# Windowed attention before a mixture of experts: scores computed in quarters of the tensor array, and a step of the attention rearranged

## The chip, the cores and the metric

The kernel runs on one core of a Trainium2 chip. The metric is the device time of one execution in microseconds (us). The engines are named as the profile names them: PE is TensorE (PEld are its weight loads), DVE is VectorE, ACT is ScalarE, POOL is GpSimd, and SP issues most of the DMAs. Each engine works through its own queue in order; an instruction that has to wait holds up everything behind it on its engine. Matmul results go to PSUM, which has eight banks of 128 partitions x 512 float32.

## What is computed

An attention with a causal window of 64 positions (8 batches, 8 heads, 576 positions, 64 features a head) is followed by a mixture of eight experts, of which each token takes one:

```python
scores = scale * np.matmul(q, k.transpose(0, 1, 3, 2))
rel = pos[:, None] - pos[None, :]
mask = (rel >= 0) & (rel < window)
scores = np.where(mask, scores, -1000000000.0)
attn = np.exp(scores - np.max(scores, axis=-1, keepdims=True))
attn = attn / (np.sum(attn, axis=-1, keepdims=True) + 1e-09)
out = np.matmul(attn, v)                      # -> x: 4608 tokens x 512
...
logits = x @ w_gate + modality_bias[modality_id]
e_idx = np.argmax(logits, axis=1)             # one expert of 8 for a token
...
h = np.maximum(x[mask] @ w1[e], 0.0)          # 512 -> 1024
out[mask] = gate_w[mask, None] * (h @ w2[e])  # 1024 -> 512
```

## The kernel before, in words

**Tiling.** The 4608 tokens are 72 blocks of 64 tokens; three blocks are a group (24 groups). The main loop (L922) has one step g for each block, and a few more to drain what is under way; `j` is g modulo 3. In each step several blocks are at different stages: `scores` of block g, `probs_t` (transposed probabilities) of block g - 1, `values` (probabilities times v) of block g - 2, and `x_t` (the result's rows transposed, for the gate) of block g - 3. Once in a group come `logits` and `logits_sum` (j = 0) and the ranks of the tokens among their experts (`route2`, `route3`, j = 2), after which the rows go to a table in DRAM, sorted by expert.

**The order is written out by hand.** Every engine gets its instructions in the order in which the loop's functions issue them. Small VectorE instructions for tables and routing wait in lists and go out one at a time where the loop calls `tick`.

**Transposed heads.** For a group, `load_qk` fetches q and k in four parts (K0, K1, Q0, Q1: k or q, first or last four heads), with two neighbouring tokens of a head beside each other, which is a run of 512 bytes in DRAM. `heads_t` transposes a part with four products into a bank `tp`. `heads_out` copies it out in two instructions of 64 partitions x 384, one for even and one for odd tokens. Parts of the next group are done while the present one is computed; the tuple `PARTS` (L467) says in which step.

**Scores.** q goes to `qbd`, where two heads stand on the diagonal of a 128x128 matrix and the rest is zero (cleared once, L826). One product of full size with `kT` then gives the scores of two heads over the window's 128 keys (L545, four products a step; each is two instructions for float32). VectorE adds the mask, scales, and takes the row minima (L551, four times); ScalarE takes the exponentials with their sums (L563, four times, two of them early in the step and two at its end).

**Banks of PSUM.** `ps_t` has two banks (`tp`: transposed heads, logits, ranks), `ps_s`, `ps_p` and `ps_a` one each (`sp` scores, `pp` transposed probabilities, `ax` values in its first 256 columns and transposed rows in the last 256), and `ps_m` three (`em`, `y0`, `y1`), which belong to the experts. As long as no expert's work is under way, odd steps borrow `em` for the scores and `y1` in place of `ax` (`spare_bank`, L473).

**The experts' work.** A slot is 256 tokens of one expert; its work is cut into sixteen pieces of TensorE (`slot_pieces`): transposes of the rows (`x_part`), products with w1 (`first`) and with w2 (`second`). From step 23 on (FIRST) each step of the attention does two pieces (`gap`), so the rest of the attention and the first slots share TensorE; behind the attention the remaining slots run alone. What a piece leaves in PSUM is taken out by entries of the list `later`, which `run_later` issues; a relu on ScalarE (L285) and a subtraction on VectorE (L286) for a pair of `first`, a split into two parts (L190, L191) for `x_part`, a scaling by the gate (L307) for the last `second`. Inside the attention `bank` gives `em` to all but the second `x_part` of a slot, which takes a `tp` bank, or `em` too where `busy` is set (j = 0).

Of the kernel before, what the change touches and what calls it, by code (L numbers as in the profile page):

```python
# [26 lines left out]
def tile_window_attn_moe(  # L27
# [24 lines left out]
    TP = 2 * P          # tokens of a slot  # L52
# [21 lines left out]
    XBUF = 9  # L74
    LG = HP * GT // 2  # column of the logits in a bank behind transposed heads
# [13 lines left out]
    # source chunks of an expert's weights, each [128, WCH] in the layout of Whi/Wlo  # L89
# [6 lines left out]
    def load_piece(raw, ev, c):  # L96
        """Columns c of an expert's weights (ev: its index, a register value)."""
# [21 lines left out]
    routing = []        # goes first  # L119

    hold = []           # VectorE has something more urgent

    def tick(n=1, table=False):
        for _ in range(0 if hold and not table else n):
# [31 lines left out]
    def tiles_of(pool, nm, c, up, size):  # L156
        """floor(c / size), or with up ceil, of whole numbers."""
# [6 lines left out]
    # experts X and Y: one-hot, first block (less DUMMY), index  # L164
# [4 lines left out]
    def first_max(pool, nm, c, out=None):  # L169
        """One-hot of the first maximum of c [1, E], and E minus its index."""  # L170
# [10 lines left out]
    def per_expert(pool, nm, c, xs_=slice(0, 2)):  # L181
        """Numbers c [1, E] of X and Y."""
# [3 lines left out]
    # ---------------------------------------------------------------- expert slots  # L186
    chunk_cols = [a * HALF + u * P for a in range(2) for u in range(HP // 2)]
# [26 lines left out]
    busy = [False]      # banks of ps_t are wanted soon  # L214
# [707 lines left out]
    for g in range(NBLK + 6):  # L922
# [56 lines left out]
        if n_gap > 2:  # L979
            gap(it)  # L980
# [285 lines left out]
```

## Time and profile before

| | us |
|---|---|
| median of 3 runs | 694.17 (694.06 to 695.51) |
| span of the profiled execution, first to last instruction | 692.6 |
| TensorE busy in the span | 670.0 |
| VectorE busy | 418.2 |
| ScalarE busy | 324.9 |

The profile records one execution; its span begins with the first instruction and ends with the last, and the time of a run also holds what lies around it. Busy times are sums over all stages, and a matmul's recorded duration contains the latency of the array, so matmuls that follow each other closely overlap in the record. In a row of the timeline stand the start, the duration, the engine, the line, the operation with its output and inputs, the shapes, how many instructions were merged, and in brackets how long the engine sat idle before and who released it. In a row of a group stand, behind the shapes and the count, the busy time in us, the mean of one in ns, and the idle time before with its releasers. In the list of who waited for whom a row gives the total in us, the number of waits and the longest.

### The profile page before, as it was taken

The numbers are of one execution on the slowest core, as the hardware profiler recorded it, in microseconds if no ns is written. First come the engines' busy times: TensorE is split into PE (matmuls) and PEld (weight loads), VectorE is DVE, ScalarE is ACT, GpSimd is POOL, SyncE is SP. The second block draws the span as 40 slices with busy tenths as digits, with TensorE's granted clock in tenths as the row PEclk, the third lists the DMA queues.
The fourth block names the chain that finished last, engine by engine and source line by source line (L and its number), as shares of the span: only waits on it lengthen the run. The fifth ranks groups of instructions, "written<-read, shape, count | busy, mean of one in ns | idle before, by whom it ended". The sixth has DMA issues, their size and how long they took to land. (4 is left out here: it accounts for less than half of the span.)

```text
span 692.6 us, 16517 instructions
## 1 busy us (share of the span) xinstructions
PE 670.0 (97%) x5814; PEld 598.9 (86%) x5814; DVE 418.2 (60%) x1760; ACT 324.9 (47%) x1029; POOL 189.3 (27%) x355
## 2 busy tenths in 40 slices
PE   7989699999999999999999999999999999999996
PEld 5778579989899898899999889999999999899985
DVE  4899987788778676675665665222226222656621
ACT  5778776666665555555555511111115211555511
POOL 6125544454454332232221251100110011111101
PEclk9999989999999999999999999999999999999998
DMA  7777896665765544554443121820505050686400
GB/s 180 182 193 203 218 234 166 175 168 160 203 177 157 145 127 131 131 153 130 130 126 83 67 78 62 278 62 32 183 31 183 32 183 31 198 258 199 143 9 34
DMA packets 108184, 97.60 MB, mean 141 GB/s; under 512 B 44602, under 2 KB 81540, under 8 KB 107972
## 3 DMA queue, kind: packets, MB, share of 16 engines
q1 hardware_dynamic: 101668, 77.51, 41.0%
q0 software_dynamic: 6432, 19.03, 7.7%
q8 instruction: 46, 0.75, 0.5%
q14 instruction: 38, 0.31, 0.2%
HBM read 67.65 MB, written 24.08 MB: 132 GB/s over the span
## 5 line engine op out<-in xcount | busy, mean ns | idle before, releaser
L563 ACT ACTIVATE ss<-ss,mn 128x128 f32<-128x128 f32 x288 | 113.4, 398 | 17.3 <-DVE mn L551 16.1
L299 PE MATMUL y<-Whi,hh 128*128 128x512 f32 x288 | 119.3, 414 | 0.0
L299 PE MATMUL y<-Whi,hl 128*128 128x512 f32 x288 | 113.7, 395 | 0.0
L299 PE MATMUL y<-Wlo,hh 128*128 128x512 f32 x288 | 113.0, 392 | 0.0
L719 POOL DMA_INDIRECT xs_scratch<-xa,idx x72 | 70.9, 984 | 141.2 <-issue 83.6
L277 PE MATMUL em<-xh,Whi 128*128 128x256 f32 x392 | 101.7, 292 | 0.0
L310 POOL DMA_INDIRECT out_dram<-y,id x36 | 37.1, 1031 | 220.4 <-DVE y L307 171.4
L277 PE MATMUL em<-xh,Wlo 128*128 128x256 f32 x392 | 96.6, 279 | 0.0
L285 ACT ACTIVATE hh<-em 128x512 fp32r<-128x512 f32 x49 | 29.3, 598 | 128.8 <-PE em L277 128.8
L286 DVE SCALAR_TENSOR_TENSOR hl<-em,hh 128x512 fp32r<-128x512 f32 x49 | 33.9, 691 | 90.4 <-ACT hh L285 90.2
L277 PEld LDWEIGHTS em<-xh,Whi 128*128 128x128 f32 x392 | 73.7, 188 | 2.3
L577 ACT COPY pT<-pp 128x512 f32<-128x512 f32 x72 | 42.1, 584 | 70.0 <-PE pp L571 69.6
L277 PEld LDWEIGHTS em<-xh,Wlo 128*128 128x128 f32 x392 | 73.7, 188 | 0.9
L545 PE MATMUL sp<-kT,qbd 128*128 128x128 f32 x488 | 66.4, 279 | 3.7 <-DVE qbd L523 3.6
L299 PEld LDWEIGHTS y<-Whi,hl 128*128 128x128 f32 x288 | 54.0, 188 | 12.6
L545 PEld LDWEIGHTS sp<-kT,qbd 128*128 128x128 f32 x488 | 59.8, 193 | 5.6 <-DVE qbd L523 4.6
L277 PE MATMUL em<-xl,Whi 128*128 128x256 f32 x392 | 62.1, 280 | 0.0
L299 PEld LDWEIGHTS y<-Whi,hh 128*128 128x128 f32 x288 | 54.1, 188 | 8.1
L299 PEld LDWEIGHTS y<-Wlo,hh 128*128 128x128 f32 x288 | 54.2, 188 | 7.6
L551 DVE CUSTOM_DVE_ANT_0 ss<-sp,masks 128x128 f32<-128x128 f32 x244 | 57.8, 279 | 4.8 <-PE sp L545 3.9
L111 POOL TENSOR_TENSOR Wlo<-raw,Whi 128x512 fp32r<-128x512 f32 x32 | 41.2, 1289 | 70.2 <-ACT Whi L110 69.9
L529 DVE COPY kT<-tp 64x384 f32<-64x384 f32 x94 | 52.1, 555 | 6.9 <-PE tp L511 4.3
(265 smaller groups left out, 1341.1 us busy)
## 6 DMA issues: line engine op xcount, KB each, us to landing
xt<-xs_scratch SPq DMA_DIRECT2D x18, 520.0 KB, 4.2
qk<-in_k_dram SPq DMA_DIRECT2D x48, 192.0 KB, 3.2
qk<-in_q_dram SPq DMA_DIRECT2D x48, 192.0 KB, 3.0
ve<-vo SPq DMA_DIRECT2D x71, 128.0 KB, 3.6
vo<-in_v_dram SPq DMA_DIRECT2D x32, 256.0 KB, 3.8
raw<-in_moe_w_dram SPq DMA_DIRECT2D x32, 256.0 KB, 2.9
vo<-in_moe_w_dram SPq DMA_DIRECT2D x24, 256.0 KB, 3.5
xs_scratch<-xs_scratch SPq DMA_DIRECT2D x8, 520.0 KB, 6.6
```

The source lines that it names most:

```text
L111: lo_engine.tensor_tensor(out=Wlo[:, buf, cols], in0=raw, in1=Whi[:, buf, cols].bitcast(F32), op=ALU.subtract)
L277: nc.tensor.matmul(out=hb[:, i * TP:(i + 1) * TP], lhsT=w[:, buf, c0:c0 + P], rhs=x[:, c * TP:(c + 1) * TP], start=(n == 0), stop=(n == le ...
L285: nc.scalar.activation(out=hh, in_=hb, func=AF.Relu),
L286: nc.vector.scalar_tensor_tensor(out=hl, in0=hb, scalar=0.0, in1=hh.bitcast(F32), op0=ALU.max, op1=ALU.subtract)))
L299: nc.tensor.matmul(out=sl["y", t], lhsT=h[:, i * TP + t * P:i * TP + (t + 1) * P], rhs=w[:, buf, c0:c0 + DM], start=(k == 0 and n == 0), s ...
L310: ins = nc.gpsimd.indirect_dma_start(out=out, out_offset=bass.IndirectOffsetOnAxis(ap=sl["id"][:, t:t + 1], axis=0), in_=y, in_offset=None ...
L529: (nc.scalar.copy if ((nm, a), t) in SCALAR or a and G == 0 else nc.vector.tensor_copy)(out=dst, in_=sv.rearrange("d (h i) -> d h i", h=HP))
L545: nc.tensor.matmul(out=sp[:, hp * P:(hp + 1) * P], lhsT=qbd[:, 1 + j if G % 2 else 2 - j, hp, :], rhs=win[:, hp], start=True, stop=True)
L551: nc.vector.tensor_tensor_reduce(out=ss[:, hp, :], in0=sp[:, hp * P:(hp + 1) * P], in1=mask, scale=-1.0 / 8.0, scalar=3.0e38, op0=ALU.add, ...
L563: nc.scalar.activation(out=ss[:, hp, :], in_=ss[:, hp, :], func=AF.Exp, bias=mn[:, hp:hp + 1], scale=-1.0, accum_out=sm[:, hp:hp + 1])
L577: nc.scalar.copy(out=pT, in_=pp)
L719: ins = nc.gpsimd.indirect_dma_start(out=xs_half, out_offset=bass.IndirectOffsetOnAxis(ap=idx[:, j:j + 1], axis=0), in_=xg[j], in_offset=None)
```

## The change

- **Scores.** `qbd` and its clearing go; q is kept in `qT` as k is in `kT`. `scores` issues eight products of 64 partitions by 64 columns, each in a quarter of the array: the partition half `a` of the operands (four of the eight heads stand in each) chooses the rows and one of two banks, `c` the columns. The product of a head takes half the partitions of the output, so the scores of two heads again fill 128 partitions. `ps_s` has two banks for it; in odd steps before the slots it borrows `y0` and `y1`.
- **Transposed heads.** `load_qk` fetches all heads of q or of k for a group into one tile, by four DMAs with runs of 256 bytes, one for each token parity and each half of the heads. `heads_t` transposes pairs of heads (one of each half), and `heads_out` copies a part out in one instruction of 128 partitions x 384 in place of two of 64.
- **Banks.** `ps_t` has one bank in place of two. Before the slots `tp_bank` takes turns between it and `em`. `ax` always has the bank of `ps_a`. The second `x_part` of a slot takes `em` as the first does.
- **Order of a step.** A step now begins with logits (j = 2), `values` and `values_out` of block g - 2, then the ranks (j = 1), `scores`, `probs_t`, all four exponentials, the first piece, the transposed heads, `x_t` and `x_t_out` of the same block g - 2, the second piece, and the second part of transposed heads. The loop is one step shorter. The device that held small VectorE instructions back (`hold`) goes, and `tick` is called with other counts.
- **Buffers.** Eight buffers `xa` in place of nine, three tiles of q and k in place of four of half the size, two in place of three of some small tables. The order of the features in the result's rows changes with the order of the heads (`chunk_cols`, `logits`).

```diff
-    ps_t = actx.enter_context(tc.tile_pool(name="ps_t", bufs=2, space=PSUM))
+    ps_t = actx.enter_context(tc.tile_pool(name="ps_t", bufs=1, space=PSUM))
...
-    qbd = att.tile([P, GB + 1, HP, P], F32, name="qbd")
+    qT = att.tile([P, HP, 6, W64], F32, name="qT")
...
-    SCALAR = ((Q0, 0), (Q0, 1))
-    LOADS = (0, 1, 1, 2)
-    HOLDJ = (2,)
-
-    def spare_bank(g):
-        """The slots' banks serve every other block as long as there is no slot."""
-        return g % 2 and g < FIRST - 1
+    SCALAR = (Q1,)
+    LOADS = (0, 1)
+
+    def early(g):
+
+        return g < FIRST - 1
+
+    n_tp = [0]
+
+    def tp_bank(g):
+        n_tp[0] += early(g)
+        if n_tp[0] % 2 and early(g):
+            return ps_m.tile([P, 512], F32, name="em")
+        return ps_t.tile([P, 512], F32, name="tp")
...
+        t = work.tile([GT // 2, HP, 2, 2, D], F32, name="qk", bufs=3)
+        src = (q_v if nm == "q" else k_v)[b, n]
+        for i in range(2):
+            for a in range(2):
+                nc.sync.dma_start(out=t[:, :, i, a, :], in_=src[:, a * HP:(a + 1) * HP, i])
...
+        src = qk[G, nm]
+        for h in range(2):
+            for t in range(2):
+                n = 2 * h + t
+                turn(tp[:, n * 96:(n + 1) * 96], src[:, 2 * i + h, t].rearrange("p a d -> p (a d)"))
...
+        dst = (qT if nm == "q" else kT)[:, 2 * i:2 * i + 2, pos0:pos0 + GB, :]
+        (nc.scalar.copy if (nm, i) in SCALAR or G == 0 and nm == "q" else nc.vector.tensor_copy)(
+            out=dst.rearrange("p h j (i t) -> p h t (j i)", t=2),
+            in_=tp[:, 0:4 * 96].rearrange("p (h t i) -> p h t i", h=2, t=2))
+        tick()
...
-        for hp in range(HP):
-            nc.tensor.matmul(
-                out=sp[:, hp * P:(hp + 1) * P], lhsT=qbd[:, 1 + j if G % 2 else 2 - j, hp, :], rhs=win[:, hp],
-                start=True, stop=True)
+        for s in range(2):
+            for a, c in ((0, 0), (1, 1), (0, 1), (1, 0)):
+                rows = slice(a * W64, (a + 1) * W64)
+                hp = 2 * c + s
+                nc.tensor.matmul(
+                    out=sp[a][c * W64:(c + 1) * W64, s * P:(s + 1) * P], lhsT=qT[rows, hp, p0, :],
+                    rhs=kT[rows, hp, p0 - 1:p0 + 1, :] if p0 else kT[rows, hp, 5::-5, :],
+                    start=True, stop=True)
```

The step's order after the change:

```diff
+        G2 = (g - 5) // GB if j == 2 else -1
+        R = (g - 7) // GB if j == 1 else -1
+        if G2 >= 0:
+            lt = tp_bank(g)
+            logits(G2, lt)
+        ax = ps_a.tile([P, 512], F32, name="ax")
+        if 2 <= g < NBLK + 2:
+            new_x(g - 2)
+            values(g - 2, ax)
+            values_out(g - 2)
+        if G2 >= 0:
+            logits_sum(G2, lt)
+            route1(G2)
...
+            tp = tp_bank(g)
+            rk = route2(R, tp)
...
+        if g < NBLK:
+            scores(g)
...
+        if 1 <= g <= NBLK:
+            probs_t(g - 1)
+            probs_out(g - 1)
+        if g < NBLK:
+            exps(g, range(HP))
+        if n_gap > 0:
+            gap(it, True)
+        part, part2 = PARTS[j]
+            heads_out(heads_t(G + 1, *part, tp_bank(g)), G + 1, *part)
...
+        if 2 <= g < NBLK + 2:
+            x_t(g - 2, ax)
+            x_t_out(g - 2, ax)
         if n_gap > 1:
             gap(it)
+        tick(2)
         if more and part2:
+            heads_out(heads_t(G + 1, *part2, tp_bank(g)), G + 1, *part2)
```

More of the change, by code (lines that the diff above doesn't have):

```diff
@@ L119, in tile_window_attn_moe @@
     routing = []
-    hold = []
     def tick(n=1, table=False):
-        for _ in range(0 if hold and not table else n):
+        for _ in range(n):
             if routing and not table:
@@ L247, in x_part @@
                     return
-            tp = ps_t.tile([P, 512], F32, name="tp") if i and not busy[0] else bank(2)
+            tp = bank(2)
             cs_ = range(2 * i, 2 * i + 2) if nb == 2 else range(NC1)
@@ L544, in scores @@
-        for hp in range(HP):
-            nc.tensor.matmul(
-                out=sp[:, hp * P:(hp + 1) * P], lhsT=qbd[:, 1 + j if G % 2 else 2 - j, hp, :], rhs=win[:, hp],
-                start=True, stop=True)
+        if g % 2 and early(g):
+            sp = [ps_m.tile([P, DM], F32, name=f"y{a}") for a in range(2)]
+        else:
+            sp = [ps_s.tile([P, 512], F32, name=f"sp{a}") for a in range(2)]
+        for s in range(2):
[6 more added lines that the diff above has]
+                    start=True, stop=True)
@@ L840, in tile_window_attn_moe @@
     nc.gpsimd.memset(masks[:, 1, 0, :], NEG)
+    nc.gpsimd.tensor_copy(out=ident_r, in_=ident)
     nc.gpsimd.memset(first_oh, 0.0)
@@ L927, in tile_window_attn_moe @@
         more = G + 1 < NG and g < NBLK
-        if j in HOLDJ:
-            hold.append(True)
-        if g < NBLK:
-            scores(g)
-            exps(g, (0, 1))
-        busy[0] = j == 0 and g < NBLK + 6
-        if n_gap > 0:
-            gap(it, True)
-        busy[0] = False
-        part, part2 = PARTS[j]
-        tp = heads_t(G + 1, *part) if more and part else ps_t.tile([P, 512], F32, name="tp")
-        G2 = (g - 6) // GB if j == 0 else -1
+        G2 = (g - 5) // GB if j == 2 else -1
+        R = (g - 7) // GB if j == 1 else -1
         if G2 >= 0:
-            lt = ps_t.tile([P, 512], F32, name="tp")
+            lt = tp_bank(g)
             logits(G2, lt)
-        R = (g - 8) // GB if j == 2 else -1
+        ax = ps_a.tile([P, 512], F32, name="ax")
[6 more added lines that the diff above has]
+            route1(G2)
         cnt = None
         if R >= 0:
+            tp = tp_bank(g)
             rk = route2(R, tp)
@@ L948, in tile_window_attn_moe @@
                 cnt = counts(R, tp)
+        if g < NBLK:
+            scores(g)
+        if R >= 0:
+            if cnt is not None:
+                cnt = counts_out(tab if R in (0, NG - 1) else pl, cnt)
+            route3(R, rk)
+        if 1 <= g <= NBLK:
[6 more added lines that the diff above has]
+        part, part2 = PARTS[j]
         if more and part:
[L950 to L953 removed]
+            heads_out(heads_t(G + 1, *part, tp_bank(g)), G + 1, *part)
         if 1 <= g <= NBLK:
@@ L956, in tile_window_attn_moe @@
             tick()
[L957 to L960 removed]
+        run_later()
+        tick(2)
         if 1 <= g <= NBLK:
             sums_inverse(g - 1)
[L963 to L966 removed]
         if 2 <= g < NBLK + 2:
[L968 to L973 removed]
+            x_t(g - 2, ax)
+            x_t_out(g - 2, ax)
         if n_gap > 1:
             gap(it)
[L976 to L994 removed]
+        tick(2)
+        if more and part2:
+            heads_out(heads_t(G + 1, *part2, tp_bank(g)), G + 1, *part2)
         for raw, n, c in raws:
@@ L1001, in tile_window_attn_moe @@
             raws.append((load_piece(raw, evs[n], c), n, c))
-        tick()
+        tick(4)
         if g == 1:
             select_bias()
-            nc.gpsimd.tensor_copy(out=ident_r, in_=ident)
         if g == 2:
```

149 lines of the change are left out of this document (46 added, 103 removed).

## The prediction

> **What bounds the kernel now.** The share of busy time comes first, then the windows by stage, because a step of the attention means one thing before the experts' pieces begin and another beside them.
>
> ```profile
> PE 670.0 (97%) x5814; PEld 598.9 (86%) x5814; DVE 418.2 (60%) x1760; ACT 324.9 (47%) x1029; POOL 189.3 (27%) x355
> ...
> 70.00:90.00 20.00, 15.05 (x171) 12.72 (x170) 18.10 (x104) 14.27 (x53) 10.09 (x13) 0.87 0.89 219
> ...
> 230.00:260.00 30.00, 30.00 (x310) 27.32 (x309) 21.98 (x99) 16.81 (x59) 10.90 (x20) 1.00 0.41 121
> ```
>
> TensorE is busy 97% of the span. The windows' columns are PE, PEld, DVE, ACT, POOL, clock, DMA share, GB/s. In the first 96 us (steps 0 to 22, no pieces; stage B below) VectorE holds 18.1 of 20 us and TensorE waits; from step 23 (stage C) TensorE never stops. Behind the attention (stage D) it does the pieces alone. The timeline of TensorE then gives the steps; a step starts with its scores (L545).
>
> ```profile
> 14.70 1.10 PE L545 MATMUL sp<-kT,qbd 128*128 128x128 f32 x8
> ...
> 73.19 1.16 PE L545 MATMUL sp<-kT,qbd 128*128 128x128 f32 x8 [1.16 <-DVE qbd L523]
> ...
> 74.61 0.53 PE L633 MATMUL tp<-xaT,wg 128*32 128x192 f32 x8
> 75.07 0.69 PE L600 MATMUL ax<-ve,pT 128*64 128x64 f32 x16
> 75.69 0.66 PE L571 MATMUL pp<-ident,ss 128*128 128x128 f32 x4
> ...
> 76.49 0.52 PE L644 MATMUL tp<-sel,part 128*64 128x8 f32 x6
> 76.94 1.16 PE L545 MATMUL em<-kT,qbd 128*128 128x128 f32 x8
> ...
> 95.74 1.08 PE L545 MATMUL sp<-kT,qbd 128*128 128x128 f32 x8
> ```
>
> Steps 2 to 22 take 95.74 - 14.70 = 81.0 us, 3.86 each. Where TensorE stands still there, the last thing it waits for is VectorE's copy of q into `qbd` (1.16 us at 73.19). In stage C a step is full:
>
> ```profile
> 253.22 1.06 PE L545 MATMUL sp<-kT,qbd 128*128 128x128 f32 x8
> 254.03 0.36 PE L277 MATMUL em<-xh,Whi 128*128 128x256 f32 x1
> ...
> 255.53 0.49 PE L511 MATMUL tp<-ident,qk 96*128 96x96 f32 x4
> 255.95 0.69 PE L600 MATMUL ax<-vo,pT 128*64 128x64 f32 x16
> ...
> 258.09 0.60 PE L571 MATMUL pp<-ident,ss 128*128 128x128 f32 x4
> 258.53 0.38 PE L617 MATMUL ax<-ident,xa 128*128 128x128 f32 x2
> 258.75 0.49 PE L511 MATMUL tp<-ident,qk 96*128 96x96 f32 x4
> 259.08 1.08 PE L545 MATMUL sp<-kT,qbd 128*128 128x128 f32 x8
> ```
>
> From start to start: scores 0.81, a piece 1.50, heads 0.42 or 0.33, probabilities 0.44, transposed rows 0.22; stage C has 49 steps (23 to 71).
>
> **The change, part by part.** *Scores.* Eight instructions of 128x128 weights (0.81 / 8 = 0.10 us each) become sixteen of 64x64 weights that stream as many columns. One after another they take 16 x 0.10 = 1.62 us; four at a time 0.41. No row has quarters; the nearest is the values' product, sixteen instructions with 64-column weights in two halves of the columns: 75.07 to 75.69, 0.62 us. I take 0.60 and keep 0.41 and 1.62 for the range. Stage C would win 0.21 x 49 = 10.3 us.
>
> The Trainium skill, TensorEngine Tiling (Array Packing), section Theoretical Speedup, allows a factor of two for each dimension of at most 64, which would be the 0.41 and a total 13 us below mine. Its section Key Properties says that a change of tiling mode drains TensorE, which speaks the other way. No run here shows either.
>
> *Copies of q and k.* Eight copies of 64x384 a group become four of 128x384: VectorE loses three of six at 0.56 us, ScalarE one of two at 0.51 (rows below). In stage B that takes about 0.56 us a step off VectorE, the present bound. What is late next is the order of the step.
>
> *The loop through ScalarE in stage B.* Now odd steps put `ax` into another bank (`spare_bank`) and the copy `xaT` stands before half of the exponentials. After the change there is one bank `ax`, its step begins with `values` into it and ends with `x_t_out` reading it, and ScalarE comes to `x_t_out` only behind `probs_out` and all four exponentials. `probs_out` waits for `probs_t`, which TensorE issues behind `values` and `scores`. So `values` of the next step waits for this step's `xaT`: a loop of one step. That waits go by bank and not by columns shows in who waited for whom:
>
> ```profile
> DVE xa L608 <- ACT xaT L624: 36.0, 31, 2.5
> ...
> DVE qbd L523 <- PE tp L690: 9.1, 9, 1.0
> ```
>
> L608 and L624 both only read `ax`, in different columns, and still one waits for the other; L690 writes columns of `tp` that L523 doesn't read. The durations:
>
> ```profile
> 41.12 0.66 PE L571 MATMUL pp<-ident,ss 128*128 128x128 f32 x4
> ...
> 41.81 0.59 ACT L577 COPY pT<-pp 128x512 f32<-128x512 f32 x1 [0.52 <-PE pp L571]
> ...
> 46.90 0.39 ACT L563 ACTIVATE ss<-ss,mn 128x128 f32<-128x128 f32 x1
> ...
> 47.29 0.39 ACT L563 ACTIVATE ss<-ss,mn 128x128 f32<-128x128 f32 x1
> ```
> ```profile
> L529 DVE COPY kT<-tp 64x384 f32<-64x384 f32 x94 | 52.1, 555 | 6.9 <-PE tp L511 4.3
> L624 ACT COPY xaT<-ax 128x256 f32<-128x256 f32 x62 | 23.6, 380 | 2.3 <-PE ax L617 2.3
> L523 ACT COPY qbd<-tp 64x384 f32<-64x384 f32 x46 | 23.3, 506 | 0.3
> ```
>
> An exponential follows the one before by 0.39, and a handover costs about 0.03 (41.12 + 0.66 to 41.81). Loop: values 0.62 + scores 0.60 + probabilities to their end 0.66 + `pT` 0.59 + four exponentials 1.56 and the last sum's read 0.10 (estimate) + `xaT` 0.38 + four handovers 0.12 = 4.63 us. The step j = 1 adds the rank's products, about 0.2 (82.36 to 82.55 below); j = 2 adds logits 0.46, their sum 0.45, and Q1's copy on ScalarE, 0.51, in front of `xaT`. A group is 3 x 4.63 + 0.2 + 1.42 = 15.5 us; the first has no logits yet, 14.4. Six of the one and one of the other: 107.4 us against 81.0, **26 us more**. VectorE (about 9 us a group: 18.1/20 of 11.6 less 1.7) and TensorE lie inside it.
>
> *Banks in stage C.* There the loop is shorter than TensorE's own work (3 x 4.63 against 5.2 and more a step) and costs nothing. But `ps_t` has one bank, and two places need it back at once. First, Q0's transposes end step j = 1 and the next step opens with `logits` into the same bank, which waits for VectorE's copy of Q0. The rows that it stands behind:
>
> ```profile
> L285 ACT ACTIVATE hh<-em 128x512 fp32r<-128x512 f32 x49 | 29.3, 598 | 128.8 <-PE em L277 128.8
> L286 DVE SCALAR_TENSOR_TENSOR hl<-em,hh 128x512 fp32r<-128x512 f32 x49 | 33.9, 691 | 90.4 <-ACT hh L285 90.2
> L307 DVE TENSOR_SCALAR y<-y,gate 128x512 f32<-128x512 f32 x36 | 27.0, 749 | 3.7 <-PE y L299 3.2
> L190 ACT CAST xh<-tp 128x512 fp32r<-128x512 f32 x28 | 16.4, 585 | 20.9 <-PE tp L252 20.7
> L191 DVE TENSOR_TENSOR xl<-tp,xh 128x512 fp32r<-128x512 f32 x28 | 19.3, 689 | 18.9 <-ACT xh L190 18.9
> ```
>
> Alone the copy holds TensorE for 0.49 - 0.33 + 0.56 + 0.07 = 0.79 us. Where the step's second piece ends a pair of `first`, VectorE does `hl` before it, behind `hh`: 0.17 + 0.60 + 0.69 + 0.56 + 0.1 - 0.33 = 1.8, with a tick 1.9; behind a result `y` 1.2. Of the steps 25, 28, ... 67 six, two and seven are of these kinds (pieces go by eight steps, groups by three): 11.4 + 2.4 + 5.5 = **19.3 us more**. Second, a slot's second transposes now go to `em`, which the next slot's first product needs. ScalarE splits them behind four exponentials: from the next start after the probabilities 0.2 + 0.59 + 1.66 + 0.59 + 0.69 + 0.06 = 3.8 us, while TensorE has some 2.5 (four transposes, a piece 1.5, heads 0.42, rows 0.22): 1.3 x 6 slots = **7.6 us more**. Stage C together: 19.3 + 7.6 - 10.3 = +16.6.
>
> *The rest.* q and k arrive in 256-byte runs instead of 512, twice as many packets.
>
> ```profile
> q1 hardware_dynamic: 101668, 77.51, 41.0%
> ```
>
> A packet of this queue holds an engine 0.41 x 692.6 x 16 / 101668 = 45 ns on average; 512 more a step cost between nothing and 512 x 45 / 16 = 1.4 us of the DMA. From 70 to 90 us, 0.89 of the time is used, and the three steps from 73.19 to 86.69 are 4.5 us each: 4.0 us a step, at most 5.4 then, against the loop's mean of 15.5 / 3 = 5.2. So the loop hides it, all but the upper bound's 0.2 x 12 steps. Eight issues in place of four in front of the first transposes: I put 0.7 us. The halved `ps_t` behind the attention: 0.1 x 11 slots = 1. The dropped clearing of `qbd` and the smaller buffers stand on POOL beside other work: nothing.
>
> **Sum.** 692.6 + 26.4 + 16.6 + 1.7 = 737.3 us of span; the median lies 1.6 above the span: **739 us**, slower.
>
> **Rivals.** *The clock falls in stage B.* TensorE would stand still for about 1.9 us a step and 2.6 in j = 2. The trace has a gap of that size:
>
> ```profile
> 82.36 0.17 PE L686 MATMUL tp<-oh,tri 64*64 64x24 bf16 x1 [0.93 <-DVE oh L670]
> ...
> 82.55 0.69 PE L600 MATMUL ax<-ve,pT 128*64 128x64 f32 x16
> ...
> 83.66 0.38 PE L617 MATMUL ax<-ident,xa 128*128 128x128 f32 x2
> 86.69 2.07 PE L545 MATMUL em<-kT,qbd 128*128 128x128 f32 x8 [2.65 <-DVE qbd L523]
> ```
>
> Behind 2.65 us of waiting the scores took twice their 1.06 and the window's clock is 0.87; behind 1.16 (73.19) nothing happened. Half speed costs the loop about 0.62 + 0.60 = 1.2 us: once a group +8 (747), in every step +25 (764). Chance 0.2. The Trainium skill, TensorE: Matmul & The Clock Gate, section What's actually happening, halves the clock after an idle window of 3.4 us; by that rule 2.6 us would not do, and the row at 86.69 says that it may.
>
> *Quarters overlap by columns only* (two at a time): scores 0.81, stage C wins nothing and the loop grows 0.2: 739 + 10 + 4 = 753, chance 0.12. *They don't overlap* (the change doesn't do what it says): 1.62, 739 + 50 + 21 = 810, chance 0.05.
>
> *The other side: `ax` is free by columns.* If `values` doesn't wait for `xaT`, the loop opens and stage B goes at VectorE's and ScalarE's work, about 9 us a group: 7 x 9 - 81 = -18 instead of +26, so 695, and 686 with quarters at 0.41. It decides at one point: whether TensorE starts `values` before `xaT` has ended. For it: the new tile's first columns were read long before. Against it: the two waits above. Chance 0.09.
>
> **How the numbers follow.** Forecast 0.5, clock 0.2, columns only 0.12, no overlap 0.05, free by columns 0.09, something else 0.04. Scores at 0.41 give 726 (the cheaper loop, too), and a bank wait of half its price in stage C about 13 less; so the low end is 712. The high end, 768, takes in the clock and the pairs; left out are the 810 and the other side. Measurement tells 0.2%: faster 0.08, same 0.04, slower 0.88.
>
> **What would show it.** In the changed profile: TensorE's `values` in steps 2 to 22 released by ACT `xaT`, steps of 4.6 to 6 us there; `logits` released by VectorE's copy of `qT` in stage C; a slot's first product into `em` released by `xl`; sixteen score instructions in 0.6 us. The prediction is wrong if stage B's steps are under 4 us, or if stage C's mean step (6.0 now) falls.

## The result and the profile after

The changed kernel takes 770.92 us (median of 4 runs, 769.75 to 777.61), the kernel before beside it 694.81 (694.06 to 695.51). The ratio is 1.1114, with a 95% interval of 1.1068 to 1.116: slower, as forecast, and 2.9 us above the high end of the range. The profiled execution took 769.75, its span is 768.0. In two of the experiments below one execution far above the others of its kernel is left out (840.83 us with the rows of x first, 1549.48 with Q1's copy on VectorE). From the page of the changed kernel (span; busy time of the engines; granted clock in 40 slices of the span; the queue of the loads):

```profile
span 768.0 us, 17641 instructions
PE 685.0 (89%) x6390; PEld 587.5 (77%) x6390; DVE 374.3 (49%) x1689; ACT 311.0 (40%) x1004; POOL 186.8 (24%) x353
PEclk9888757799998989999989899999999999999999
q1 hardware_dynamic: 140068, 77.51, 38.4%
```

TensorE went from 97% busy to 89% of a longer span: it now waits. The granted clock, 0.992 in the mean before, is 0.934: it lies at 0.5 to 0.8 from the second slice to the eighth (19 to 154 us) and dips to 0.8 four times more up to the twenty-third. The loads make 140068 packets in place of 101668 and take 38.4% of the DMA engines' time in place of 41.0%. Of the longer span that is more (0.384 x 768.0 = 295 us against 284), but of TensorE's waits only 2.0 us go back to these loads, all of it before step 2.

The starts of the scores of steps 2, 23 and 71 bound the stages, in the timeline of TensorE in the changed kernel (scores are now L548, values L604):

```profile
15.46 0.67 PE L548 MATMUL sp<-kT,qT 64*64 64x128 f32 x16
...
134.04 1.13 PE L548 MATMUL sp<-kT,qT 64*64 64x128 f32 x16
...
457.52 0.67 PE L548 MATMUL sp<-kT,qT 64*64 64x128 f32 x16
```

Before, steps 2 and 23 stand in the prediction, and step 71 is this row:

```profile
385.12 1.06 PE L545 MATMUL sp<-kT,qbd 128*128 128x128 f32 x8
```

| us | before | predicted | after |
|---|---|---|---|
| start to step 2 | 14.7 | 15.4 | 15.5 |
| stage B, steps 2 to 22 | 81.0 | 107.4 | 118.6 |
| stage C, steps 23 to 70 | 289.4 | 306.0 | 323.5 |
| behind the start of step 71 | 307.5 | 308.5 | 310.5 |

Stage B is 11.2 us and stage C 17.5 us longer than predicted; that is nearly all of the 31 us that are missing in the span. (Between the two bounds stage C holds 48 steps; the prediction spoke of 49.) The waits of TensorE in the changed kernel, in all (total, number, longest), show the three mechanisms that the prediction named:

```profile
PE ax L604 <- ACT xaT L627: 29.9, 18, 2.5
PE tp L635 <- DVE qT L529: 22.8, 16, 2.2
PE em L274 <- DVE xl L189: 7.3, 6, 1.5
```

A step of stage B, in TensorE's timeline of the changed kernel:

```profile
35.88 0.69 PE L604 MATMUL ax<-ve,pT 128*64 128x64 f32 x16 [2.47 <-ACT xaT L627]
36.49 0.67 PE L548 MATMUL sp<-kT,qT 64*64 64x128 f32 x16
37.09 0.66 PE L432 MATMUL pp<-ident,ss 128*128 128x128 f32 x4
...
40.27 0.69 PE L604 MATMUL ax<-vo,pT 128*64 128x64 f32 x16 [1.98 <-ACT xaT L627]
...
41.21 1.11 PE L548 MATMUL y<-kT,qT 64*64 64x128 f32 x16
```

The values wait for ScalarE's copy `xaT`, as forecast; scores in quarters take 37.09 - 36.49 = 0.60 us; a step with ranks at full clock takes 41.21 - 36.49 = 4.72. But the scores at 41.21 are recorded with 1.11, not 0.67, and the transposes behind them follow after 1.04 instead of 0.60: the clock has halved. The same in stage C, around two waits for Q0's copy:

```profile
232.60 0.87 PE L635 MATMUL tp<-xaT,wg 128*32 128x192 f32 x8 [2.19 <-DVE qT L529]
...
234.99 1.13 PE L548 MATMUL sp<-kT,qT 64*64 64x128 f32 x16
...
239.10 0.48 PE L296 MATMUL y<-Whi,hl 128*128 128x512 f32 x1
...
256.46 0.53 PE L635 MATMUL tp<-xaT,wg 128*32 128x192 f32 x8 [1.82 <-DVE qT L529]
```

Behind 2.19 us of waiting everything takes nearly twice its time until 239.1, 6.5 us long, which costs some 3 us beside the wait; behind 1.82 us the logits take their 0.53 and nothing happens. So this wait, which the prediction priced at 1.9, cost more than five. But its length alone doesn't decide. Two more waits for Q0's copy in this kernel, and two windows around them (behind a window's length stands the busy time of TensorE):

```profile
318.21 0.53 PE L635 MATMUL tp<-xaT,wg 128*32 128x192 f32 x8 [2.19 <-DVE qT L529]
...
319.62 0.67 PE L548 MATMUL sp<-kT,qT 64*64 64x128 f32 x16
...
416.19 0.53 PE L635 MATMUL tp<-xaT,wg 128*32 128x192 f32 x8 [1.84 <-DVE qT L529]
...
418.18 1.13 PE L548 MATMUL sp<-kT,qT 64*64 64x128 f32 x16
```
```profile
314.34:317.75 3.41, 1.69 (x16) 1.50 (x14) 2.18 (x14) 1.04 (x4) 0.00 (x0) 1.00 0.61 149
413.34:416.75 3.41, 1.57 (x17) 0.94 (x18) 2.58 (x11) 0.29 (x2) 1.22 (x3) 1.00 0.79 189
```

Behind this 2.19 the scores go at full speed, and behind this 1.84 at half. The record of the granted clock in the trace tells why: every change in it lies on a grid of 3.41 us, in each of the eighteen traces, and the two windows are cells of the grid. The 1.84 us lie within one cell, which has 3.41 - 1.57 = 1.84 us of idling; a border of the grid (317.76) cuts the other wait, and the cell before the border has 3.41 - 1.69 = 1.72. Over all eighteen traces, each of the 140 cells at full clock with 1.84 us of idling or more was followed by half clock. From 1.29 to just under 1.84 us both happened, and below that the clock fell once. Of the six waits of 2.19 us five were followed by half clock, four of them for two cells, and of the two of 1.8 us one.

### The profile page after: what moved, and what is told of

It is laid out like the page before. It is cut to its first block, busy times and chain, and to the rows that moved or that the text cites. A ratio compares the mean times of both kernels' runs of the same rounds, so it can differ in the third digit from the quotient of the medians.

```text
span 768.0 us, 17641 instructions
## 1 busy us (share of the span) xinstructions
PE 685.0 (89%) x6390; PEld 587.5 (77%) x6390; DVE 374.3 (49%) x1689; ACT 311.0 (40%) x1004; POOL 186.8 (24%) x353
## 3 DMA queue, kind: packets, MB, share of 16 engines
q1 hardware_dynamic: 140068, 77.51, 38.4%
## 4 chain that ended last, share of the span: by engine, by line
PE 76%; ACT 13%; DVE 6%; issue 3%; DMA 1%; SPq 1%; POOL 0%; ACTq 0%; POOLq 0%; DVEq 0%
PE y L296 22%; PE em L274 17%; PE pp L274 7%; ACT ss L566 7%; PE ax L604 6%; PE pp L432 6%; PE sp L548 5%; ACT pT L580 2%; PE tp L432 2%; PE tp L635 1%; DVE qT L529 1%; DVE xl L189 1%; PE ax L432 1%; ACT hh L282 1%; PE y L548 1%
## 5 line engine op out<-in xcount | busy, mean ns | idle before, releaser
L296 PE MATMUL y<-Whi,hh 128*128 128x512 f32 x288 | 121.8, 423 | 0.0
L612 DVE TENSOR_TENSOR xa<-ax,rs 128x256 f32<-128x256 f32 x72 | 30.3, 421 | 77.5 <-PE ax L604 72.6
L556 DVE CUSTOM_DVE_ANT_0 ss<-sp,masks 128x128 f32<-128x128 f32 x244 | 56.1, 284 | 22.8 <-PE sp L548 22.4
L432 PE MATMUL pp<-ident,ss 128*128 128x128 f32 x288 | 57.3, 329 | 0.2
L566 ACT ACTIVATION_READ_ACCUMULATOR ss<-ss,mn 128x1 f32 x288 | 54.5, 189 | 0.0
```

Source lines behind the costliest of these rows:

```text
L296: nc.tensor.matmul(out=sl["y", t], lhsT=h[:, i * TP + t * P:i * TP + (t + 1) * P], rhs=w[:, buf, c0:c0 + DM], start=(k == 0 and n == 0), s ...
L432: nc.tensor.transpose(out=out_, in_=in_, identity=ident[0:n, 0:n])
L556: nc.vector.tensor_tensor_reduce(out=ss[:, u, :], in0=sp[a][:, s * P:(s + 1) * P], in1=mask, scale=-1.0 / 8.0, scalar=3.0e38, op0=ALU.add, ...
L566: nc.scalar.activation(out=ss[:, hp, :], in_=ss[:, hp, :], func=AF.Exp, bias=mn[:, hp:hp + 1], scale=-1.0, accum_out=sm[:, hp:hp + 1])
```

## Experiments

Theory A: the waits of the rearranged step, each with the time at half clock that follows it, are the whole loss, and the quarters are a gain. Rivals: the clock costs nothing where ScalarE sets the pace anyway; the waits overlap, so that one takes the place of another; the quarters themselves cost.

The first four changed one place each, and are compared with the 770.92 above; before beside them gave 695.72. The changed kernel itself did not run beside them. In its place stand the stages that an edit leaves alone: stage B takes 117.2 and 120.5 us in the second and third of them (118.6 above), stage C 320.2 and 318.9 in the first and fourth (323.5 above), so a few us decide nothing. **Rows of x first:** in steps below 23 `x_t` and `x_t_out` come ahead of the exponentials.

```diff
+        if g < FIRST and 2 <= g < NBLK + 2:
+            x_t(g - 2, ax)
+            x_t_out(g - 2, ax)
         if g < NBLK:
             exps(g, range(HP))
```

> The changed kernel with one edit: in steps below 23, x_t and x_t_out stand before the four exponentials instead of behind them; everything is still computed. Theory A (the loop through ScalarE bounds the first stage: values waits for xaT, xaT for four exponentials): the loop loses the exponentials' 1.66 us, steps fall from 118.6 / 21 = 5.6 us to about 3.5 (then probabilities 0.66 + pT 0.59 + xaT 0.38 + exponentials 1.66 + handovers), so the stage takes some 76 us in place of 118.6 and the kernel 771 - 42 = 729 us (722 to 740); the waits of values for xaT all but go. Theory B (the stage is bound by the packets of 256 bytes, or by VectorE): the stage stays above 110 us and the kernel above 762.

736.5 us (731.6 to 739.7), ratio 1.0553 (1.0501 to 1.0605). Stage B falls from 118.6 to 91.6, stage C stays (320.2). The wait for `xaT` shrinks, and a new one appears, here in the waits and the timeline of this kernel:

```profile
PE ax L604 <- ACT xaT L627: 6.0, 15, 0.7
```
```profile
42.87 0.66 PE L548 MATMUL y<-kT,qT 64*64 64x128 f32 x14 [0.87 <-ACT qT L529]
```

Once a group the scores now wait 0.87 us for Q1's copy, which stands behind the exponentials on the same engine. So the loop through ScalarE held stage B, and 27 us of the 37.6 come back by order alone.

**Q0 ahead of the second piece** (steps from 23 on), so that VectorE copies Q0 while TensorE does the piece:

```diff
         if n_gap > 1:
+            if more and part2:
+                heads_out(heads_t(G + 1, *part2, tp_bank(g)), G + 1, *part2)
             gap(it)
         tick(2)
-        if more and part2:
+        if more and part2 and n_gap < 2:
```

> The changed kernel with one edit: from step 23 on the second part of transposed heads (Q0) is issued before the second piece instead of behind it; everything is still computed. In the changed trace logits waited 22.8 us in 16 places for the copy of Q0, and the granted clock is below 1 in parts of the second stage. Theory A (the bank wait costs its length, and about as much again because the clock falls behind waits of 2.2 us): these waits go, some 0.4 us a group comes back as a wait for the copy of K1, the clock of the second stage goes to 0.98 or more, and the kernel wins 28 to 36 us (735 to 743). Theory B (the wait costs only its length, the clock falls for another reason): 13 to 19 us won (752 to 758), the clock of the second stage stays near 0.93. Theory C (the wait is taken over by something else): less than 5 us.

744.21 (742.96 to 747.67), ratio 1.0715 (1.0678 to 1.0752): 26.7 us won, just short of the 28 to 36 expected, but more than the 22.8 of the waits, and these are not all gone. From this kernel's waits and windows (the windows' columns as in the prediction, the clock is the third number from the end):

```profile
PE tp L432 <- DVE kT L529: 9.1, 16, 1.6
```
```profile
160.00:200.00 40.00, 37.73 (x462) 32.04 (x459) 23.19 (x127) 22.58 (x79) 18.18 (x26) 1.00 0.64 170
```

Stage C falls by 26.2 us, its waits in all by 13.4; the other 12.8 us go with the clock, which is 1.00 from 160 us on.

**Exponentials behind the first piece** (steps from 23 on: `exps` moves from in front of the first `gap` to behind it).

> The changed kernel with one edit: from step 23 on the exponentials are issued behind the first piece, so that the split of a slot's second transposes stands before them on ScalarE; everything is still computed. Theory A (the next slot's first product waits 1.15 us in 6 places because the split stands behind four exponentials): these waits go, 6 to 9 us won (762 to 765). Theory B (it waits because the two x_parts share em, whatever ScalarE's order): the waits stay, under 2 us won.

761.11 (759.57 to 761.83), ratio 1.0934 (1.0914 to 1.0955): 9.8 us won, a little more than the 6 to 9 expected, and the waits of 1.15 us for `xl` go. This is the second rearrangement that the prediction priced, at 7.6.

**Idle products in stage B.** Four products of the identity with the masks at the end of steps 1 to 22 keep TensorE at work while it waits; nothing else moves.

```diff
+        if 1 <= g < FIRST:
+            for _ in range(4):
+                nc.tensor.matmul(out=st["sp"][:, 256:512], lhsT=ident,
+                                 rhs=masks.rearrange("p a s c -> p (a s c)"), start=True, stop=True)
```

> The changed kernel with one addition: in steps 1 to 22 four products of the identity with the masks (256 columns, about 0.43 us each at full clock) are issued at the step's end into unused columns of a bank of scores, so that TensorE idles less than 1 us a step; their result is not used. Theory A (the first stage lost some 11 us beyond the loop to a clock that falls behind idle times of 2 to 2.5 us): the clock there stays at 1.0, the steps return to the loop's 4.7 to 5.9, the stage takes 107 us in place of 118.6 and the kernel 757 to 763. Theory B (the clock is not granted for other reasons, or the stage's excess lies in the loop itself): the stage stays at 116 us or more and the kernel at 768 or more.

751.66 (749.45 to 754.71), ratio 1.0801 (1.0754 to 1.0847): work added, 19 us won, where 757 to 763 was expected. Two windows of the changed kernel, then the same two of this one:

```profile
75.00:100.00 25.00, 18.76 (x216) 15.19 (x213) 13.49 (x82) 12.73 (x48) 10.99 (x16) 0.71 0.64 160
100.00:134.00 34.00, 23.47 (x280) 18.31 (x278) 19.61 (x116) 19.04 (x72) 13.64 (x17) 0.70 0.73 172
```
```profile
75.00:100.00 25.00, 22.86 (x275) 18.14 (x273) 18.44 (x96) 15.92 (x60) 12.08 (x15) 1.00 0.73 187
100.00:134.00 34.00, 28.25 (x361) 22.83 (x357) 22.71 (x120) 19.55 (x74) 14.92 (x20) 1.00 0.75 183
```

At full clock stage B takes 106.4 us; the prediction's loop gave 107.4. The half clock cost 12.2 us there. Stage C, without such products, is 4.6 us shorter too; in the changed kernel its first 9.6 us still run at the half clock that stage B leaves behind.

**All three orders together**, then with **Q1's copy on VectorE** below step 23 in addition, **idle products in stage C** (one to four at the end of the steps g mod 3 = 1), and **the quarters by bank**, on another chip:

```diff
-            for a, c in ((0, 0), (1, 1), (0, 1), (1, 0)):
+            for a, c in ((0, 0), (0, 1), (1, 0), (1, 1)):
```

> The three reorderings that won alone, together: rows of x transposed ahead of the exponentials in steps 2 to 22, Q0 transposed ahead of the second piece and the exponentials behind the first piece from step 23. Theory A (the waits of the rearranged step and the clock that falls behind the longest of them account for everything lost; quarters are cheaper scores): the wins add, 770.9 - 32.8 - 26.7 - 9.8 = 702, range 694 to 712, stage B 90 to 92, stage C 283 to 291, clock 1.00 from 160 us on. Rival (the wins overlap: each removes the same half-clock stretches, about 12 us of them counted twice): 712 to 722, stage C 295 or more.

> The same, and Q1 is copied by VectorE instead of ScalarE in the groups below step 23, so that the scores no longer stand 0.87 us behind ScalarE's exponentials and copies once a group. Theory: 6 or 7 groups by 0.9, and where the clock fell behind it (54.4 to 58 us of the rows-first run) some 3 to 6 more: 6 to 12 us under the run without it, stage B about 81 to 85, time 690 to 700. Rival (VectorE, with the most work of this stage beside TensorE, hands the wait on to the copies of K0 and Q0 or to the reads of the scores): within 3 us of the run without it.

> The changed kernel with 1 to 4 idle products of 0.24 us each (8 took 1.89) at the end of the steps g mod 3 = 1 from step 23 on, four ahead of the six waits of 2.19; the order and every wait's end are as they were. Theory A (TensorE's clock halves behind a wait of 2.19 us and stays so for about 6.5 us, which costs some 3.2 us each beside the wait; 1.82 us do not do it): stage C falls from 323.5 by 10 to 17 us, the steps behind the waits take scores of 0.60, clock near 1.00 from 160 us on, time 752 to 761. Rival (the loss of the stage is waits alone): stage C within 3 us of 323.5, time 768 to 773.

> The changed kernel with the four quarters of a set of scores in the order of their banks, (rows 0, columns 0), (0, 1), (1, 0), (1, 1), instead of diagonal first. Theory A (quarters that differ in rows and in columns run beside each other; in neighbours that share rows or columns the second waits): the 16 products take more than 0.60, between 0.60 and 1.2, and the time rises by up to 0.6 x 70 = 42 us in the steps that TensorE bounds; taken 0.80, +10 to +14 us. Rival (16 products of 0.037 us go out one behind the other at a fixed pace whatever quarter they take): 0.60 as before, time within 3 us of the changed kernel's.

None of the four times came out. All three orders: 739.83, ratio 1.0565 (1.0515 to 1.0616), not 694 to 712. With Q1's copy on VectorE: 733.3 (729.14 to 737.93), ratio 1.0477 (1.0396 to 1.0559); only its distance, 6.5 us less, is as that theory had it, and stage B is 89.3 in place of 97.1, not 81 to 85. Idle products in stage C 798.11, ratio 1.1382 (1.134 to 1.1424), quarters by bank 799.14, ratio 1.1423 (1.1384 to 1.1462), 27 and 28 us *above* the changed kernel, and equal. Before stood at 699.46 there. The sixteen score instructions by bank took 0.60 us as before (207.74 to 208.34 in its timeline), so their order counts for nothing.

Two different edits that give one time call for a control. It ran on a third chip, beside one part of the change undone (**two `ax` banks** by turns in steps 0 to 21, for which the scores no longer borrow `y0` and `y1` and always take the banks of `ps_s`), that with two of the orders, and the idle products once more:

```diff
-        ax = ps_a.tile([P, 512], F32, name="ax")
+        if g % 2 and early(g):
+            ax = ps_m.tile([P, DM], F32, name="y0")
+        else:
+            ax = ps_a.tile([P, 512], F32, name="ax")
```

> The changed kernel itself, once more, beside the three others. In the runs with the quarters by bank and with idle products in the pieces, ScalarE and VectorE stand still for about 2 us once a group of three steps, which the first run of the changed kernel does not show, and both came out at 798. Theory A (that comes from where those ran, not from their edits): the changed kernel gives 770 to 778 without these stalls, or 795 to 800 with them, and the others of this call have them or lack them alike. Rival (the edits made them): 768 to 778 here while the run with the idle products shows the stalls again.

> One part undone: values and transposed rows of x take the ax bank and the y0 bank by turns in steps 0 to 21, as before the change (scores take sp always, as in the stage behind). Theory A (the loop values - rows of x - ScalarE's copy behind the exponentials - values, through the one bank, is what stage B lost): stage B falls from 118.6 to 80 to 92, no wait of the values for xaT there, clock 0.95 or more, and the time by 27 to 38 us beside the changed kernel of this call. Rival (ScalarE's and VectorE's order in the step holds it anyway): stage B 105 or more.

> Two ax banks, Q0 transposed ahead of the second piece, the exponentials behind the first piece. Theory A (bank loop, Q0's bank and the second transposition of an expert's rows, each with the clock it costs, are the whole loss, and scores in quarters are a gain): 30 + 26.7 + 9.8 us under the changed kernel, about 704 where that gives 771, range 694 to 714. Rival (order of the step costs beside the banks): 715 or more.

> The kernel with idle products at the end of the steps g mod 3 = 1 again, now beside the changed kernel itself. Theory A (the clock halves behind waits of about 2.2 us; four products of 0.24 ahead of each of the six leave 1.2): 10 to 17 us under the changed kernel of this call. Rival: within 3 us of it.

The changed kernel itself took 798.74 here (797.04 to 799.39), ratio 1.1362 (1.1322 to 1.1401), before 703.58. So the 28 us belong to where it ran and not to the edits. Two `ax` banks give 770.18, ratio 1.095 (1.0909 to 1.0991), 28.6 less than the control, and stage B 104.3 in place of 126.9; of the waits for `xaT` the logits' 7.4 us are nearly all that is left there, yet it is not the 80 to 92 that were expected: the values now wait 9.9 us for `pT` and the scores 4.4 for Q1's copy. With the orders 750.57, ratio 1.0672 (1.0613 to 1.073), 48 less instead of 66. Idle products 798.02, ratio 1.1375 (1.1321 to 1.1429).

What holds these runs up shows in the control's timeline (from its second run, below, on this chip; GpSimd, TensorE, VectorE, ScalarE), and then at the same place in the first run of the changed kernel:

```profile
187.01 0.98 POOL L721 DMA_INDIRECT xs_scratch<-xa,idx  x1 [0.28 <-issue]
...
187.91 0.65 PE L432 MATMUL pp<-ident,ss 128*128 128x128 f32 x4
...
188.39 0.42 DVE L612 TENSOR_TENSOR xa<-ax,rs 128x256 f32<-128x256 f32 x1 [2.63 <-PE sp L548]
188.46 0.97 POOL L721 DMA_INDIRECT xs_scratch<-xa,idx  x1 [0.28 <-POOL xa L720]
189.20 0.17 DVE L650 TENSOR_TENSOR lg<-tp,bias_sel 64x24 f32<-64x24 f32 x1 [0.39 <-PE pp L432]
...
189.94 0.29 DVE L556 CUSTOM_DVE_ANT_0 ss<-sp,masks 128x128 f32<-128x128 f32 x1 [0.56 <-PE pp L432]
190.09 0.59 ACT L580 COPY pT<-pp 128x512 f32<-128x512 f32 x1 [3.29 <-PE pp L432]
```
```profile
176.10 0.42 DVE L612 TENSOR_TENSOR xa<-ax,rs 128x256 f32<-128x256 f32 x1 [1.34 <-PE tp L635]
176.49 0.17 DVE L650 TENSOR_TENSOR lg<-tp,bias_sel 64x24 f32<-64x24 f32 x1
...
176.91 0.66 PE L432 MATMUL pp<-ident,ss 128*128 128x128 f32 x4
...
177.03 0.29 DVE L556 CUSTOM_DVE_ANT_0 ss<-sp,masks 128x128 f32<-128x128 f32 x1 [0.37 <-PE sp L548]
...
177.66 0.59 ACT L580 COPY pT<-pp 128x512 f32<-128x512 f32 x1 [1.85 <-PE pp L432]
```

From `xa` to the first read of the scores VectorE takes 1.55 us in the control and 0.93 in the first run, and ScalarE starts `pT` 1.5 us behind the end of the transposes (188.56) in place of 0.1, while GpSimd hands out the three scatters of a group. The scatters themselves take 0.98 us in both. In the first control it recurs nearly every group, by up to 2.6 us; in the first run of the changed kernel no start of `pT` is late by over 0.1, and in the first four experiments none by over 0.4. Is it theirs, and does before have it? **Scatters spread** hands them out one at a time with the routing's other work; **all together** has two `ax` banks, the three orders, Q1 on VectorE and the spread scatters.

```diff
-            for j in range(GB):
-                scatter(j)
         routing.append(rows)
+        for j in range(GB):
+            routing.append(lambda j=j: scatter(j))
```

> The changed kernel, as the control of this call: 769 to 778 where ScalarE's copy of pT starts within 0.1 us of the end of the transposes throughout, 795 to 800 where it is about 2 us late once a group of three steps.

> The kernel before, profiled beside it. Theory A (the stalls belong to the scatters, which both kernels have, and before hides them better): where the control stalls, this shows ScalarE or VectorE late by 1 to 2 us beside its scatters too, and it gives 699 to 704; without stalls 694 to 696. Rival (only the changed kernel makes them): no such gaps here while the control has them.

> The changed kernel with the three scatters of a group handed out one by one through the routing work instead of in a row. Theory A (each scatter holds up ScalarE and VectorE while GpSimd works on it, and three in a row make the 2 us): where the control stalls, gaps of 0.5 to 1 us at three places in the place of one of 2, part of them hidden, and 5 to 20 us less; without stalls within 4 us of the control. Rival (the stalls have another cause): as the control, gaps of 2 us as before.

> Two ax banks in steps 0 to 21, rows of x ahead of the exponentials there, Q0 ahead of the second piece, exponentials behind the first piece, Q1 by VectorE below step 23, scatters spread. Theory A (all causes of the loss are named, and scores in quarters gain 0.21 us a step in the stage that TensorE bounds): 690 to 706 without stalls, 705 to 735 with them. Rival (something of the rearranged step is left): 710 or more without stalls, 735 to 745 with them.

The control again 796.46, ratio 1.1377 (1.1341 to 1.1413). Before, profiled: 699.52, ratio to itself 1.0002 (0.9982 to 1.0022), and it has the stalls too, here in the timeline of before on that chip (TensorE, GpSimd, ScalarE):

```profile
346.60 0.60 PE L571 MATMUL pp<-ident,ss 128*128 128x128 f32 x4
...
346.98 0.98 POOL L719 DMA_INDIRECT xs_scratch<-xa,idx  x1 [0.28 <-issue]
...
350.06 0.58 ACT L577 COPY pT<-pp 128x512 f32<-128x512 f32 x1 [5.48 <-PE em L277]
...
351.43 0.69 PE L600 MATMUL ax<-ve,pT 128*64 128x64 f32 x16 [1.06 <-DVE xa L608]
```

The transposes had ended at 346.60 + 0.60 = 347.20, so `pT` is 2.9 us late; TensorE loses 1.06 us at this place, and stage C in all about 1 us (290.3 against 289.4). In the changed kernel the same lateness of ScalarE makes the values wait for `xaT`: 14.3 us of such waits in stage C of the first control, 0.8 in the first run. Spread scatters give 783.99, ratio 1.1234 (1.1163 to 1.1304), 12.5 us less than the control; from 75 to 300 us no start of `pT` is late by over 1 us (the control has four there, by 1.5 to 2.2), and behind that, where three scatters still follow each other at 1.5 us, most that are late are so by 1.8 to 2.5 as before. Not all of the gain need come from this: of the 18.8 us between the two spans 7.1 lie in stage B, where the control's copies are late by at most 0.4. All together: 722.76, ratio 1.0341 (1.0297 to 1.0385), 74 us less than the control, stage B 86.8 against before's 84.7 on that chip, and stage C 306.6 against 290.3, in which TensorE still waits 26.0 us, 11.8 of them for `xaT`. Before is faster still; without the late copies this version was not measured.

Issuing each scatter twice, which would have doubled the suspected cause, was not tried, since both writes go to the same rows. No version that beats the kernel before was found.

## Why the prediction was too low

The direction and the three mechanisms that it counted were right. The step that failed is the price of a wait of TensorE: the sum counts its length and puts the half clock behind it at nothing. The prediction had the clock as a rival for stage B alone, with a chance of 0.2, and behind the waits of stage C not at all. The runs showed some 12 us of it in stage B and 13 in stage C. That the time came out only 2.9 us above the range is partly luck of the place: where the copies are late the same kernel takes 796 to 799, and nothing in the prediction covers that. An account of stage C: length, TensorE's waits in it (the sum of all rows of the waits between the stage's bounds), and the difference, which is its work. For the changed kernel the rows are, with 32.8 us in all:

```profile
PE tp L635 <- DVE qT L529: 22.1, 15, 2.2
PE em L274 <- DVE xl L189: 5.8, 5, 1.2
PE em L249 <- DVE xl L189: 2.3, 1, 2.3
PE tp L432 <- DVE tgt L702: 1.3, 2, 0.7
PE ax L604 <- ACT xaT L627: 0.8, 3, 0.4
PE ax L432 <- DVE e_take L133: 0.5, 1, 0.5
```

| stage C, us | length | waits | work |
|---|---|---|---|
| before | 289.4 | 1.6 | 287.8 |
| after | 323.5 | 32.8 | 290.7 |
| Q0 ahead of the second piece | 297.3 | 19.4 | 277.9 |
| control, third chip | 343.2 | 50.5 | 292.7 |
| idle products there | 335.2 | 37.6 | 297.6 |

Before's work less the forecast gain of the scores is 287.8 - 10.3 = 277.5. With Q0 ahead of the second piece and the granted clock at 0.99 over the stage, the work is 277.9: **the gain of the quarters is real, and of the predicted size.** After, it is 290.7, 13.2 us more, at a granted clock of 0.93. That these are half clock is what a subtraction leaves, but the other runs bear it out: over the fourteen changed kernels without idle products in stage C, the work grows by about 0.7 us for each us of clock withheld there (the share not granted times the length, 21.9 us after), and a straight line through them comes to some 277 us at none withheld, an estimate.

The idle products on the third chip fit this. The 72 instructions of stage C go out every 1.89 / 8 = 0.24 us, 17 us of their own, and 297.6 - 17 = 280.6 against the control's 292.7, 12 us less at a granted clock of 0.98 in place of 0.94. (A product is two instructions; the expectation took it for one.) The waits fall by 12.9 us as well, so stage C is 8.0 us shorter. The totals, 798.02 and 798.74, don't tell, because the stretches without such products are 7 us longer in that profiled execution (stage B 130.6 against 126.9, behind the start of step 71 313.4 against 310.8). On the second chip stage C took 341.1 us with them, against 338.1 with the quarters by bank. What these products are worth in the whole stage stays open.

Point by point:

- *Loop through ScalarE, 107.4 us:* 106.4 at full clock. Right; half clock adds 12.2 for 118.6.
- *Scores at 0.60, -10.3 us in stage C:* right.
- *Q0 and the logits in one bank, 19.3 us:* the waits are 22.1, with 0.74, 1.8 and 2.19 us where it said 0.79, 1.2 and 1.9. Five of the six of 2.19 cost the clock as well, and one of the two of 1.8.
- *Second transposes in `em`, 7.6 us:* 5.8 in the stage, 7.3 in all; taken away, 9.8 us of time.
- *Not foreseen:* 2.3 + 1.3 + 0.8 + 0.5 = 4.9 us of smaller waits. All waits together grew by 31.2 us where 26.9 were predicted, 4.3 more; with the clock's 13.2 that is the 17.5 us of stage C.
- *Start 0.7, behind the attention 1:* 0.8 and 3.0. Small.
- *The other side (`ax` free by columns):* it isn't; values wait for `xaT`. By the Trainium skill, PSUM — Partial Sum Buffer, section Terms, two engines on one bank and quadrant collide. Here the wait is for the whole bank, which is also the whole tile, so the runs don't tell the two apart; with two banks by turns, and the scores in `ps_s`, stage B was 22.6 us shorter.
- *Half clock behind 2.65 us:* it takes less, and not the length of one wait but the idling within a cell of the grid counts. In the trace of before that the prediction quotes, the clock falls at 84.86, when that wait had lasted only 0.8 us; the cell that ended there held the 0.93 us of the wait before it too, 1.74 us in all. The Trainium skill, TensorE: Matmul & The Clock Gate, section What's actually happening, has a free-running window of about 3.4 us that must be idle; by that rule no wait here would have halved the clock (the longest is 2.5), and the rows show that they do: the grid of 3.41 us is there, but half a cell of idling is enough. By that rule the forecast would stay at 739; with what the rows show it is 739 + 12 + 13 = 764.

## What to carry to other kernels

A wait of TensorE has two prices, its length and, where the idle time within one cell of the clock's grid comes near 1.8 us, the half clock behind it; so two short waits close together can cost it, and a wait of 2.2 us that a border cuts need not. Price it wherever the trace has one example of it. When stages are packed onto fewer PSUM banks, follow each bank around its loop through the in-order queues of the engines that empty it: the loop's time replaces the bound, and the slack that hid lateness elsewhere goes with it. And where two unrelated edits give the same time, run the unchanged kernel beside them before explaining either.

## What the runs showed of the hardware

- The same program took 770.92, 798.74 and 796.46 us on different occasions (the latter two on one chip), while the kernel before went only from 694.81 to 703.58 and 699.54. Where it is slow, ScalarE and VectorE start up to 2.6 us late beside the scatters, and in this kernel TensorE soon waits for them. The Trainium skill, SBUF — State Buffer, section Who interferes with whom, says that ScalarE never waits on another engine's port; what delays it here stays open, and that it is the scatters rests on the spread alone, which took part of it away.
- The granted clock of TensorE changes only on a grid of 3.41 us, by all eighteen traces. Idling of 1.84 us or more in a cell was always followed by half clock (140 cells), and 1.29 to just under 1.84 us sometimes.
- Sixteen instructions on quarters of the array (64 x 64 weights, 128 columns, float32) take 0.60 us, 37 ns each, in either order of the quarters, against 0.81 for eight of full size. That is a gain of 26%, not of two.
